# Second channel product of a ReLU-squared attention and MLP-mixer kernel: from one product per token tile to seven block products per two tiles (Strassen)

## The chip, the cores and the metric

The kernel runs on one core of one Trainium2 chip. The core has TensorE (PE, matrix products from on-chip memory SBUF into the accumulator PSUM, eight banks), VectorE (DVE), ScalarE (ACT), GpSimd (POOL, which here issues the loads) and SyncE (SP, which here issues stores and the DMA transposes), and 16 DMA engines. Each engine works through its own queue in order and waits on semaphores. The metric is the device time of the whole kernel in microseconds; lower is better.

## The reference

q, k and v are 8 batches x 12 heads x 448 tokens x 64. With them the reference computes

```python
scores = scale * np.matmul(q, k.transpose(0, 1, 3, 2))     # scale = 1/sqrt(64)
attn = np.maximum(scores, 0.0) ** 2 / S                     # S = 448
x = np.matmul(attn, v), heads side by side                  # 8 x 448 x 768
h = np.maximum(x.transpose(0, 2, 1) @ w_tok1, 0.0) @ w_tok2 # token mixing, 448 -> 256 -> 448
u = x + h.transpose(0, 2, 1)
h2 = np.maximum(u @ w_ch1, 0.0) @ w_ch2                     # channel mixing, 768 -> 1536 -> 768
out = u + h2                                                # float32
```

## The kernel before

The work goes in steps s = 0 to 23, one per batch b and group of four heads (three steps per batch). All 8 x 448 = 3584 tokens make 28 token tiles of 128, seven for every two batches (bb counts these pairs of batches). The products are in bf16 with float32 accumulation.

*Attention of a step.* GpSimd loads k, q and v (`ldk`, `ldq`, `ldv`, two DMAs each) into `raws`, four buffers of each. k and q are turned by TensorE up to step 9 (`T`), and from step 10 on by DMA: VectorE copies k or q into a buffer of `sides` (`ik`, `iq`; two buffers, so a copy waits for the transpose of two steps before), and SP issues a DMA transpose from there into `kqT` (`xk`, `xq`). For each of seven chunks c of 64 keys TensorE makes scores (`S`, two banks), ScalarE or VectorE takes the relu out of the banks into one of 13 buffers `sq` (`r`), VectorE squares it in place (`q`), and TensorE adds the value product (`V`, two banks held over all seven chunks). The result goes to `xT` (`xe`).

*Token mixing of a step.* From step 5 on SP turns `xT` into `x_sb` with a DMA transpose (`xd`); TensorE makes the first product (`t1`), ScalarE its relu (`rt`), TensorE the second (`t2`), and VectorE adds x to give u (`u`), which is kept channel-first in `uT_sb`, one buffer for two batches, two buffers in turn. SP turns u with DMA transposes into `u_sb`, token-first (`ub`), for use as the residual; `ub` is left out for batch 0, whose residual TensorE adds to the product with an identity matrix (`RESPE = {0}`, L572).

*Channel mixing.* The first product (`C1.b.e`, L517) is made for one batch and one of 12 blocks e of 128 hidden channels, six matmuls of 448 columns; ScalarE writes its relu to `r2_sb` (`c1e`), which holds two batches and exists twice. The second product (`C2.bb.t.i`, L568) takes one token tile t and a half i of the 768 output channels, 12 matmuls of 384 columns in one bank, one for each e; VectorE adds `u_sb` to it into one of three `out_sb` (`c2e`, L584), and SP stores the tile in two DMAs (`st`). The last tile goes in three parts.

*What sets the order.* `ORDER` is one long list of these names. The program emits them in that order, so every engine's queue holds its own operations in the list's order; a suffix `:A` or `:D` puts a step on ScalarE or VectorE, and digits name PSUM banks. The list had been worked out ahead of time. The first channel product of the later batches and most second products serve as TensorE's work beside the attention; about 80 us at the end consist of channel products alone.

Of the kernel before, what the change touches and what calls it, by code (L numbers as in the profile page):

```python
# [7 lines left out]
BF16 = mybir.dt.bfloat16  # L8
# [4 lines left out]
HOLD = 1  # L13
NSIDE = 2
FUSED = set()
RESPE = {0}
# [44 lines left out]
ldf.0 ident ldf.1 ldk0.1 ldk0.0 ldq1.1 ldk1.0 cast0.0:D cast0.1:A wt1.0 ldv1.0 ldq1.0 cast1.0:D cast1.1:A  # L61
ldk1.1 ldk2.1 fill:1*15 T0.0:0 ldv0.1 T0.1:1 cp0.0:A ldv0.0 cp0.1:D ldq2.1 fill:4*6 S0.4:23 S0.2:45 S0.5:67
ldv1.1 r0.4.0:A r0.4.1:D S0.1:01 r0.2.0:A r0.2.1:D ldk2.0 S0.0:23 r0.5.0:A r0.5.1:D ldq2.0 S0.3:45 r0.0.0:A
q0.2:D r0.0.1:A S0.6:67 ldk4.0 q0.4:D r0.1.0:A T1.0:23 ldq4.0 r0.1.1:A r0.3.0:D r0.3.1:A ldk4.1 q0.0:D cp1.0:A
cp1.1:D ldq4.1 r0.6.0:A q0.1:D S1.2:01 V0.0:45 ldk3.1 r0.6.1:A q0.3:D V0.1 r1.2.0:A V0.2 S1.1:32 q0.5:D wt1.1
S1.0:67 r1.2.1:A V0.3 q0.6:D V0.4 r1.0.0:A ldq3.1 V0.5 S1.5:01 q1.2:D r1.0.1:A V0.6 wt2 r1.1.0:A r1.1.1:D
S1.4:67 xe0.0:A xe0.1:D ldv2.1 r1.5.0:A q1.0:D r1.5.1:A ldv2.0 T2.0:32 q1.1:D r1.4.0:A V1.0:45 ldq3.0 r1.4.1:A
q1.5:D V1.1 S1.3:01 cp2.0:A cp2.1:D ldk3.0 X0.0:6 q1.4:D r1.3.0:A S1.6:72 wc1.0 X0.1:3 r1.3.1:A xc0.0:D
xc0.1:D r1.6.0:A S2.0:06 ldk5.1 q1.3:D S2.1:13 r1.6.1:A ldq5.0 r2.0.0:A r2.0.1:D S2.5:72 V1.2 r2.1.0:A q1.6:D
V1.3 S2.3:06 r2.1.1:A V1.4 r2.5.0:D V1.5 r2.5.1:A t1.0.0:1 q2.0:D r2.3.0:A V1.6 S2.4:37 q2.1:D r2.3.1:A  # L70
T4.0:20 ldv5.0 xe1.0:A xe1.1:D ldq5.1 rt0.0:A t1.0.1:6 q2.3:D r2.4.0:A ldv3.1 S2.2:45 r2.4.1:A cp4.0:D X1.1:1
ldk5.0 rt0.1:A cp4.1:D S2.6:37 r2.2.0:A V2.0:26 ldv3.0 V2.1 xc1.1:D r2.2.1:A T3.0:04 q2.4:D r2.6.0:A q2.2:D
r2.6.1:A X1.0:1 t1.1.1:5 cp3.0:A q2.5:D V2.2 S4.2:37 q2.6:D V2.3 xc1.0:A V2.4 V2.5 cp3.1:D V2.6 rt1.1:A
r4.2.0:A t1.1.0:0 r4.2.1:D xe2.0:A t2.0.1:1 xe2.1:D t2.1.1:5 rt1.0:A u0.1:D X2.0:4 S3.4:37 xc2.0:A u1.1:D
S3.3:26 wc1.1 t2.0.0:0 r3.4.0:A r3.4.1:D X2.1:1 t2.1.0:4 r3.3.0:A ldv4.0 u0.0:D t1.2.0:5 r3.3.1:A xc2.1:D
ldq7.0 S3.5:37 u1.0:D rt2.0:A S3.6:20 S3.0:61 r3.5.0:A ldq8.0 r3.5.1:D t2.2.0:5 r3.6.0:A S3.1:43 q3.3:D ldk7.0
r3.6.1:A t1.2.1:7 u2.0:D r3.0.0:A C1.0.2a:2 ldk6.0 rt2.1:A q3.4:D r3.0.1:A t2.2.1:0 ldv5.1 q3.5:D r3.1.0:A
C1.0.0a:6 r3.1.1:A u2.1:D ldv4.1 C1.0.1a:5 q3.0:D q3.1:D C1.0.2 q3.6:D S4.4:71 c1e0.2:A S4.3:43 q4.2:D
C1.0.4:0 r4.4.0:A r4.3.0:A r4.4.1:D r4.3.1:A C1.0.0 q4.4:D c1e0.4:A S3.2:27 q4.3:D T5.0:41 c1e0.0:A r3.2.0:A
r3.2.1:D S4.1:30 C1.0.1 cp5.0:A cp5.1:D C1.0.3:6 q3.2:D c1e0.1:A r4.1.0:A r4.1.1:D ldq7.1 V3.0:27 c1e0.3:A  # L80
S5.4:14 q4.1:D V3.1 ldq6.0 S4.5:53 S5.0:06 V3.2 r4.5.0:A r4.5.1:D V3.3 ldq6.1 V3.4 r5.0.0:A V3.5 r5.0.1:D
S5.2:53 V3.6 ldk6.1 r5.4.0:A r5.4.1:D C1.0.5:0 xe3.0:A xe3.1:D ldk7.1 r5.2.0:A q5.0:D r5.2.1:A C1.0.11:6 wc2.1
q4.5:D c1e0.5:A q5.2:D wc2.0 X3.0:1 c1e0.11:A q5.4:D S4.0:42 S5.1:75 wc2.2 xc3.0:D S4.6:30 r4.0.0:A C1.0.10:6
r4.0.1:A r5.1.0:D ldv6.1 r4.6.0:A r5.1.1:D ldv6.0 r4.6.1:A t1.3.0:1 q4.0:D c1e0.10:A ldv7.1 q5.1:D C1.0.6:4
# [573 lines left out]
```

## Time and profile before

| | before |
|---|---|
| three runs, median (lowest to highest) | 369.79 us (366.51 to 371.76) |
| span of the profiled execution | 368.3 us |
| mean granted TensorE clock | 0.989 |
| DMA traffic | 49.84 MB, mean 135 GB/s |
| squares, L422, VectorE | 168 x 618 ns, 97.1 us busy |
| relus of scores, ScalarE and VectorE | 227 and 109, 108.7 and 63.8 us busy |
| output adds, L584, VectorE | 51, 27.9 us busy |
| relus of the first channel product, ScalarE | 95 x 549 ns, 52.1 us busy |
| DMA transposes by SP: u, k and q, x | 42, 28, 19 |

A busy time is the union of an engine's instructions, so a group's mean is longer than the distance between two of its instructions that follow each other at once; the distance is read from the starts in a timeline. A busy share is an average over stages with different limits, so stages are read apart.

### The profile page before, as it was taken

The numbers are of one execution on the slowest core, as the hardware profiler recorded it, in microseconds if no ns is written. First come the engines' busy times: TensorE is split into PE (matmuls) and PEld (weight loads), VectorE is DVE, ScalarE is ACT, GpSimd is POOL, SyncE is SP. The second block draws the span as 40 slices with busy tenths as digits, with TensorE's granted clock in tenths as the row PEclk, the third lists the DMA queues.
The fourth block names the chain that finished last, engine by engine and source line by source line (L and its number), as shares of the span: only waits on it lengthen the run. The fifth ranks groups of instructions, "written<-read, shape, count | busy, mean of one in ns | idle before, by whom it ended". The sixth has DMA issues, their size and how long they took to land.

```text
span 368.3 us, 8763 instructions
## 1 busy us (share of the span) xinstructions
PE 355.3 (96%) x3564; PEld 198.8 (54%) x3564; DVE 245.8 (67%) x458; ACT 189.9 (52%) x388; POOL 91.3 (25%) x156
## 2 busy tenths in 40 slices
PE   7789999999999799999999999999999999999995
PEld 4455455565655355555555555555545565555564
DVE  3996999979389575989477997988588213201222
ACT  4996888548374356746164765566366122122200
POOL 9865532415154032133033033301000000000000
PEclk9998999999999989999999999999999999999999
DMA  8999999949999979999999599999141511511435
GB/s 152 175 184 190 189 182 179 143 100 136 154 181 147 190 126 154 170 134 182 225 116 197 105 145 157 189 165 190 32 89 26 118 44 25 134 43 25 104 85 130
DMA packets 96073, 49.84 MB, mean 135 GB/s; under 512 B 69984, under 2 KB 92576, under 8 KB 96032
## 3 DMA queue, kind: packets, MB, share of 16 engines
q1 hardware_dynamic: 71440, 27.61, 42.8%
q0 software_dynamic: 24352, 21.47, 42.7%
q8 instruction: 28, 0.46, 0.5%
q10 hardware_dynamic: 240, 0.20, 0.2%
q14 instruction: 13, 0.11, 0.1%
HBM read 43.38 MB, written 11.01 MB: 148 GB/s over the span
## 4 chain that ended last, share of the span: by engine, by line
PE 90%; DMA 4%; DVE 3%; issue 1%; ACT 1%; POOL 0%; POOLq 0%; ACTq 0%
PE m_ps L517 30%; PE m_ps L568 29%; PE sc_ps L412 9%; PE acc_ps L439 9%; PE t_ps L483 6%; PE h_ps L492 5%; DMA x_sb<-xT 3%; DVE sq L422 2%; PE kqT_ps L371 1%; DMA k_raw<-in_k_dram 1%; DVE sq L251 1%; PE x_ps L474 1%; DVE kqT L257 0%; ACT sq L249 0%; PE m_ps L572 0%
## 5 line engine op out<-in xcount | busy, mean ns | idle before, releaser
L249 ACT ACTIVATE sq<-sc_ps 128x448 bf16<-128x448 f32 x227 | 108.7, 570 | 30.4 <-PE sc_ps L412 27.9
L517 PE MATMUL m_ps<-uT_sb,wc 128*128 128x448 bf16 x576 | 119.0, 353 | 0.0
L568 PE MATMUL m_ps<-wc,r_sb 128*128 128x384 bf16 (+2 forms) x684 | 117.2, 323 | 0.0
L249 ACT ACTIVATE r_sb<-m_ps 128x448 bf16<-128x448 f32 x95 | 52.1, 549 | 102.1 <-PE m_ps L517 101.9
L422 DVE TENSOR_TENSOR sq<-sq 128x896 bf16<-128x896 bf16 x168 | 97.1, 618 | 0.9 <-ACT sq L249 0.2
L568 PEld LDWEIGHTS <-r_sb 128*128 128x128 bf16 x684 | 65.6, 98 | 45.3 <-issue 2.9
L517 PEld LDWEIGHTS <-wc 128*128 128x128 bf16 x576 | 54.6, 98 | 53.2 <-issue 6.8
L584 DVE TENSOR_TENSOR out_sb<-m_ps,u_sb 128x384 f32<-128x384 f32 (+2 forms) x51 | 27.9, 548 | 72.5 <-PE m_ps L568 61.5
L251 DVE TENSOR_SCALAR sq<-sc_ps 128x448 bf16<-128x448 f32 x109 | 63.8, 618 | 16.5 <-PE sc_ps L412 8.9
L271 POOL DMA_DIRECT2D v_raw<-in_v_dram x48 | 29.2, 616 | 121.7 <-PE sc_ps L412 64.7
L412 PE MATMUL sc_ps<-kqT 64*64 64x448 bf16 x672 | 55.9, 360 | 1.9 <-ACT kqT L255 1.7
L439 PE MATMUL acc_ps<-sq,v_raw 64*64 64x448 bf16 x672 | 49.0, 362 | 1.0 <-ACT sq L249 0.4
L271 POOL DMA_DIRECT2D q_raw<-in_q_dram x46 | 28.5, 632 | 28.8 <-PE kqT_ps L371 19.9
L496 DVE TENSOR_TENSOR uT_sb<-h_ps,xT 128x448 bf16<-128x448 f32 x48 | 29.0, 618 | 8.1 <-PE h_ps L492 7.8
L412 PEld LDWEIGHTS <-kqT 64*64 64x64 bf16 x672 | 20.8, 106 | 23.0 <-issue 13.4
L271 POOL DMA_DIRECT2D k_raw<-in_k_dram x48 | 29.6, 631 | 3.0 <-DMA wc<-in_moe_w_ch_dram 1.1
L439 PEld LDWEIGHTS <-v_raw 64*64 64x64 bf16 x672 | 21.2, 109 | 14.4 <-issue 6.1
L483 PE MATMUL t_ps<-x_sb,wt 128*128 128x256 bf16 (+1 forms) x216 | 26.6, 269 | 2.4 <-DMA x_sb<-xT 2.4
L483 PEld LDWEIGHTS <-wt 128*128 128x128 bf16 x216 | 19.5, 101 | 10.1 <-DMA x_sb<-xT 2.8
L492 PE MATMUL h_ps<-wt,r_sb 128*128 128x448 bf16 x96 | 24.6, 354 | 0.0
L249 ACT ACTIVATE r_sb<-t_ps 128x512 bf16<-128x512 f32 (+1 forms) x27 | 15.5, 575 | 14.4 <-PE t_ps L483 14.3
L451 DVE TENSOR_SCALAR xT<-acc_ps 128x448 bf16<-128x448 f32 x24 | 14.8, 619 | 1.6 <-PE acc_ps L439 1.6
(39 smaller groups left out, 109.4 us busy)
## 6 DMA issues: line engine op xcount, KB each, us to landing
out_dram<-out_sb SPq DMA_DIRECT2D x54, 192.0 KB, 3.1
k_raw<-in_k_dram POOLq DMA_DIRECT2D x48, 112.0 KB, 6.2
v_raw<-in_v_dram POOLq DMA_DIRECT2D x48, 112.0 KB, 5.4
q_raw<-in_q_dram POOLq DMA_DIRECT2D x46, 112.0 KB, 6.4
wc<-in_moe_w_ch_dram POOLq DMA_DIRECT2D x2, 1152.0 KB, 10.7
wc<-in_moe_w_ch_dram POOLq DMA_DIRECT2D x3, 768.0 KB, 12.9
u_sb<-uT_sb SPq DMA_TRANSPOSE x42, 4.0
side<-in_q_dram SPq DMA_DIRECT2D x2, 224.0 KB, 3.4
```

The lines of the kernel that those rows point to most:

```text
L249: nc.scalar.activation(out, ps, AF.Relu)
L251: nc.vector.tensor_scalar(out=out, in0=ps, scalar1=0.0, scalar2=None, op0=ALU.max)
L271: nc.gpsimd.dma_start(out=raws[t][s % NR][64 * half:64 * (half + 1)], in_=src[b, h0:h0 + 2].rearrange('e (p c) d -> p e (c d)', c=KC))
L412: nc.tensor.matmul(o.ps[e][64 * half:64 * (half + 1), :S], lhsT=lhsT, rhs=rhs, start=True, stop=True, skip_group_check=True)
L422: sq_ops[s, c] = [add(Op(f'q{s}.{c}', 'DVE', lambda o: nc.vector.tensor_tensor(out=buf, in0=buf, in1=buf, op=ALU.mult), ev))]
L439: nc.tensor.matmul(o.ps[half][64 * e:64 * (e + 1), :S], lhsT=r[rows, e, c * D:(c + 1) * D], rhs=sq[rows, e, :], start=c == 0, stop=c == KC ...
L483: nc.tensor.matmul(o.ps[:, j, :], lhsT=wt1[:, c, j * 128:(j + 1) * 128], rhs=x_sb[:, p0:p1, c, :], start=c == 0, stop=c == 3)
L492: nc.tensor.matmul(o.ps[:, :S], lhsT=r1[:, j, a * 128:(a + 1) * 128], rhs=wt2[:, j, :], start=j == 0, stop=j == JC - 1)
L496: nc.vector.tensor_tensor(out=uTs[bb % 2][:, 2 * i + a, off:off + S].rearrange('n (c p) -> n c p', c=KC), in0=t2.ps[:, :S].rearrange('n (p ...
L517: nc.tensor.matmul(ps[:, :S], lhsT=wc1[:, g, e * 128:(e + 1) * 128], rhs=uT[:, g, off:off + S], start=g == 0, stop=g == CC - 1)
L568: nc.tensor.matmul(o.ps[:, :size], lhsT=r2[:, e, t * 128:(t + 1) * 128], rhs=wc2[:, e, cols], start=e == 0, stop=e == EC - 1)
L584: nc.vector.tensor_tensor(out=out_sb[:, cols].rearrange('n (g d) -> n g d', d=128), in0=u.ps[:, :size].rearrange('n (g d) -> n g d', d=128 ...
```

## The change

The second channel product takes two token tiles at a time (14 pairs p). Let A be the pair's rows of `r2`, as blocks A11, A12 (first tile; first and second half of the 1536 hidden channels), A21 and A22 (second tile), and B11 to B22 the four blocks of w_ch2, 768 x 384 each. Strassen's scheme in Winograd's form makes the four output blocks from seven products of a block by a block (`P1` to `P7`), six matmuls of 384 columns each. It needs

- four sums of blocks of A for each pair, on VectorE in bf16, 128 x 768 elements each: S1 = A21 + A22, S2 = S1 - A11, S4 = A12 - S2 in the buffers `sums`, and S3 = A11 - A21 written over A21;
- four sums of blocks of B, once, on VectorE in eight pieces (`ws`);
- seven adds into `out_sb` for each pair (`a`, `b`, `c`, `f21`, `f11`, `f22`, `f12`) where there were four. P1, P6, P7 and P4 accumulate in one bank, which VectorE reads after each of them; `a`, `b`, `c` and `f21` add u from `u_sb`, the other three add P2, P5 and P5 + P3 to what is in `out_sb`.

`r2` and `u_sb`, which were two buffers of seven tiles each, become rings of eleven tiles (`RING`). A batch whose tokens run over the ring's end is evicted in two pieces (`c1e` of batches 3 and 6), and its `ub` transposes are issued in two pieces too. The residual of batch 0 now comes through `ub` as well. To make room, `sides` goes from two to one (`NSIDE`; a copy now waits for the transpose of the step before), `sq` from 13 to 10 (`NSQ`), v's buffers from four to three; `out_sb` goes from three to four; the warm-up operand lies in an `out_sb`, and B12 in `sums`. w_ch2 is loaded in four blocks rather than three parts. `ORDER` is worked out anew, so every operation may stand at another place, and some evictions move between ScalarE and VectorE. There are 28 start-up filler matmuls where there were 21.

```diff
-HOLD = 1
-NSIDE = 2
-FUSED = set()
-RESPE = {0}
+HOLD = 3
+NSIDE = 1
+RING = 11
+NSUM = 6
...
-    NR, NQ, NSQ, NX, NO = (4, 3, 13, 3, 3)
+    EH = EC // 2
+    RT = RING * 128
+    NQ, NSQ, NX, NO = (3, 10, 3, 4)
+    NR = {'k': 4, 'q': 4, 'v': 3}
...
-    wc2 = sbuf.tile([128, EC, DM], BF16, name='wc2')
+    wc2 = {w: sbuf.tile([128, EH, HN], BF16, name=f'wc2_{w}') for w in ('11', '21', '22', 't1', 't2', 't3', 't4')}
+    sums = sbuf.tile([128, NSUM, EH, 128], BF16, name='sums')
+    wc2['12'] = sums[:, 0:3].rearrange('p a e n -> p (a e n)').rearrange('p (e n) -> p e n', e=EH)
...
-    u_sbs = [sbuf.tile([128, CC, NT, 128], BF16, name=f'u_sb{i}') for i in range(2)]
-    r2s = [sbuf.tile([128, EC, 2 * S], BF16, name=f'r2_sb{i}') for i in range(2)]
+    u_sb = sbuf.tile([128, CC, RING, 128], BF16, name='u_sb')
+    r2 = sbuf.tile([128, EC, RT], BF16, name='r2_sb')
...
+    def weight_sums():
+        for h in range(2):
+            e = slice(h * EH // 2, (h + 1) * EH // 2)
+            for w, x, y in (('t1', '12', '11'), ('t3', '22', '12'), ('t2', '22', 't1'), ('t4', '21', 't2')):
+                deps = [wc2_ops[z] if z in wc2_ops else wsum[z, h] for z in (x, y)]
+                wsum[w, h] = add(Op(f'ws{w[1]}.{h}', 'DVE', lambda o, w=w, x=x, y=y, e=e: nc.vector.tensor_tensor(out=wc2[w][:, e], in0=wc2[x][:, e], in1=wc2[y][:, e], op=ALU.subtract), deps))
...
+                for t0, t1, slot in ((lo, cut, first), (cut, hi, 0)):
+                    if t0 < t1:
+                        x = nc.sync.dma_start_transpose(out=u_sb[:, g, slot:slot + t1 - t0, :], in_=uTs[bb % 2][:, g, t0 * 128:t1 * 128])
...
+        def evict(o):
+            for x, y, z in ((0, cut, at), (cut, S, 0)):
+                if x < y:
+                    relu(o, r2[:, e, z:z + y - x], u.ps[:, x:y])
...
+        sum1 = summed('s1', s1, block(1, 0), block(1, 1), ALU.add, ready(1, 0) + ready(1, 1) + old)
+        sum3 = summed('s3', block(1, 0), block(0, 0), block(1, 0), ALU.subtract, ready(0, 0) + [sum1])
+        sum2 = summed('s2', s2, s1, block(0, 0), ALU.subtract, [sum1] + ready(0, 0) + old)
+        sum4 = summed('s4', s4, block(0, 1), s2, ALU.subtract, [sum2] + ready(0, 1) + old)
...
+                for e in range(EH):
+                    nc.tensor.matmul(banks[into][:, :HN], lhsT=lhs[:, e], rhs=wc2[w][:, e], start=after is None and e == 0, stop=e == EH - 1, skip_group_check=True)
...
+        p1 = product(1, block(0, 0), '11', ready(0, 0), 'x')
+        a = added('a', 0, 0, 'x', [p1], True)
+        p6 = product(6, s2, 't2', [sum2], 'x', a)
+        b = added('b', 0, 1, 'x', [p6], True)
+        p7 = product(7, block(1, 0), 't3', [sum3], 'x', b)
+        c = added('c', 1, 1, 'x', [p7], True)
+        p4 = product(4, block(1, 1), 't4', ready(1, 1), 'x', c)
+        f21 = added('f21', 1, 0, 'x', [p4], True)
+        p2 = product(2, block(0, 1), '21', ready(0, 1), 'y')
+        f11 = added('f11', 0, 0, 'y', [p2, a], False)
+        p5 = product(5, s1, 't1', [sum1], 'z')
+        f22 = added('f22', 1, 1, 'z', [p5, c], False)
+        p3 = product(3, s4, '22', [sum4], 'z', f22)
+        f12 = added('f12', 0, 1, 'z', [p3, b], False)
```

More of the change, by code (lines that the diff above doesn't have):

```diff
@@ L417, in score @@
         old = vals[divmod(n - NSQ, KC)] if n >= NSQ else None
-        if (s, c) in FUSED:
-            sq_ops[s, c] = [add(Op(f'z{s}.{c}.{e}', 'DVE', lambda o, e=e: nc.vector.scalar_tensor_tensor(out=buf[:, e], in0=u.ps[e][:, :S], scalar=0.0, in1=u.ps[e][:, :S], op0=ALU.max, op1=ALU.mult), [u, old])) for e in range(2)]
-            return u
         ev = [add(Op(f'r{s}.{c}.{e}', 'ACT', lambda o, e=e: relu(o, buf[:, e], u.ps[e][:, :S]), [u, old])) for e in range(2)]
```

437 lines of the change are left out of this document (223 added, 214 removed).

## Prediction

> **What bounds the kernel now.** I read the head of the page, then the chain of waits, then the busy time by stage, since the shares of the whole span average over an attention part and a tail that have different limits.
>
> ```profile
> span 368.3 us, 8763 instructions
> ...
> PE 355.3 (96%) x3564; PEld 198.8 (54%) x3564; DVE 245.8 (67%) x458; ACT 189.9 (52%) x388; POOL 91.3 (25%) x156
> ...
> PE 90%; DMA 4%; DVE 3%; issue 1%; ACT 1%; POOL 0%; POOLq 0%; ACTq 0%
> PE m_ps L517 30%; PE m_ps L568 29%; PE sc_ps L412 9%; PE acc_ps L439 9%; PE t_ps L483 6%; PE h_ps L492 5%; DMA x_sb<-xT 3%; DVE sq L422 2%; PE kqT_ps L371 1%; DMA k_raw<-in_k_dram 1%; DVE sq L251 1%; PE x_ps L474 1%; DVE kqT L257 0%; ACT sq L249 0%; PE m_ps L572 0%
> ```
>
> TensorE (PE) carries 90% of the chain, and the second channel product (L568) alone 29%: the stage that the change shortens is on the path. By stage (columns: busy time of PE, its weight loads, VectorE, ScalarE, GpSimd; granted clock; DMA share):
>
> ```profile
> 0.00:30.00 30.00, 23.54 (x502) 14.13 (x506) 22.20 (x46) 23.12 (x47) 22.18 (x41) 0.98 1.08 172
> 30.00:285.50 255.50, 252.71 (x2589) 138.56 (x2590) 206.17 (x380) 152.64 (x316) 69.13 (x115) 0.99 1.01 149
> 285.50:364.40 78.90, 78.90 (x479) 46.15 (x477) 17.06 (x31) 14.15 (x26) 0.00 (x0) 1.00 0.33 78
> ```
>
> The cut at 285.5 us is where the last x transposes (xd22, xd23) are issued. After it PE is full and VectorE has 17.06 of 78.90; before it PE is full too, but VectorE is already at 206.17 of 255.50 (81%), and the DMA engines at 1.01. So the tail has room for VectorE work, the attention part little.
>
> **The change part by part.** Rates first, from starts in PE's timeline, since a group's own duration overlaps its successor:
>
> ```profile
> 282.35 2.06 PE L439 MATMUL acc_ps<-sq,v_raw 64*64 64x448 bf16 x40
> 284.34 1.31 PE L517 MATMUL m_ps<-uT_sb,wc 128*128 128x448 bf16 x6
> ...
> 287.44 2.43 PE L517 MATMUL m_ps<-uT_sb,wc 128*128 128x448 bf16 x12
> 289.70 0.54 PE L492 MATMUL h_ps<-wt,r_sb 128*128 128x448 bf16 x2
> 290.08 7.96 PE L568 MATMUL m_ps<-wc,r_sb 128*128 128x384 bf16 x48
> 297.88 1.04 PE L483 MATMUL t_ps<-x_sb,wt 128*128 128x256 bf16 x8
> 298.76 2.43 PE L517 MATMUL m_ps<-uT_sb,wc 128*128 128x448 bf16 x12
> ```
>
> A 384-column matmul takes (297.88 - 290.08)/48 = 0.1625 us, a 448-column one (289.70 - 287.44)/12 = 0.188, a t1 group 0.88, a t2 group 0.38, and four quadrant matmuls of a V step (284.34 - 282.35)/10 = 0.20.
>
> *TensorE.* Before: 28 token tiles x 2 halves x 12 = 672 matmuls. After: 14 pairs x 7 products x 6 = 588. That is 84 x 0.1625 = 13.65 us less. The residual by identity goes, and seven start-up fills come:
>
> ```profile
> L572 PE MATMUL m_ps<-ident,uT_sb 128*128 128x128 bf16 x18 | 2.0, 219 | 0.0
> L627 PE MATMUL fill_ps<-warm 128*128 128x128 bf16 x21 | 1.5, 220 | 0.0
> ```
>
> At a third of 0.1625 a 128-column matmul is 0.054, so the 18 give 1.0 (at most the 2.0 of the row) and the fills take 0.4, in a stretch where PE waits anyway. TensorE's sum: -14.3. The order moves first channel groups too: with 20 after xd23 where there were 23 (3 x 6 x 0.188 = 3.4 us), and 42 products (42 x 6 x 0.1625 = 41.0) for 25 groups of the old form (25 x 12 x 0.1625 = 48.8), the tail is 78.9 - 11.2 = 67.7 us long. So most of the gain lies in the tail, and before xd23 PE has only 3 us less.
>
> *VectorE.* Its back-to-back rate:
>
> ```profile
> 278.36 0.55 DVE L584 TENSOR_TENSOR out_sb<-m_ps,u_sb 128x384 f32<-128x384 f32 x1
> 278.84 0.62 DVE L251 TENSOR_SCALAR sq<-sc_ps 128x448 bf16<-128x448 f32 x1
> 279.38 1.69 DVE L422 TENSOR_TENSOR sq<-sq 128x896 bf16<-128x896 bf16 x3
> ```
>
> An output add of 384 takes 0.48, a relu of 448 from PSUM 0.54, and so does a square ((1.69 - 0.62)/2). Adds go from 56 to 98: +42 x 0.48 = 20.2. The sums of r2 blocks (bf16, SBUF, 768 elements) stand in no row; the nearest is the square of 896: between 0.46 (by proportion) and 0.54, and I take 0.48: 56 x 0.48 = 26.9. Eight weight sums of 1152 elements: 0.54 x 1152/896 = 0.69 each, 5.5. Moves between VectorE and ScalarE come to -3.8. Together +48.8, of which 29.5 before xd23: (206.17 + 29.5)/255.5 = 92%, beside a PE at 98%. After it VectorE has some 35 of 67.7 us and is covered.
>
> What 92% costs two in-order engines I bound by pieces. I cut each order list into ten equal parts, count both engines' work by the rates above, and sum the larger. Before it is 342.2 (PE's own sum 334.2); after it is 335.3 (PE 319.9). In the new parts one to six VectorE leads or ties: 22.5, 27.0, 25.9, 30.8, 30.7, 30.0 against 13.5, 23.4, 24.6, 29.7, 30.7, 29.5. So of 14.3 only 342.2 - 335.3 = 6.9 is left: VectorE gives back 7.4. Bounds: 0 (it hides behind the waits that the 368.3 - 342.2 us between sum and span hold) and 14.3 (all).
>
> *The x transposes.* xd copies xT into x_sb through SP's queue, t1 on PE waits for it, and everything on PE queues behind t1.
>
> ```profile
> L462 SPq DMA_TRANSPOSE x_sb<-xT x19: 1231/1303/3438, 63.0 to 286.8; - x19
> DMA to landing us min/median/max: 3.1/6.8/13.2
> ...
> DMA to landing us min/median/max: 3.1/3.2/3.3
> ```
>
> (The last row is for 260 to 290 us, when no loads run.) In the old order the work between xd and t1, the larger of PE and VectorE, is 8.0 us at least; in the new one it is 5.9, 5.5, 5.9, 6.2, 5.4 and 5.4 for steps 5, 10, 12, 13, 17, 20. At a landing of 6.8 the shortfalls sum to 6.5; at 3.2 to nothing. The k and q loads go out earlier (from step 10 on 13 us of work or more before use, where 6.6 was the least), which thins the DMA queue at those places, but the v loads still start beside xd. I take 3, bounds 0 and 6.5 here. One such wait is in the trace:
>
> ```profile
> 116.79 10.64 DMA x_sb<-xT
> ...
> 122.64 2.43 PE L517 MATMUL m_ps<-uT_sb,wc 128*128 128x448 bf16 x12
> 127.47 1.68 PE L483 MATMUL t_ps<-x_sb,wt 128*128 128x256 bf16 x8 [2.40 <-DMA x_sb<-xT]
> ...
> 126.00:128.00 2.00, 0.53 (x4) 0.45 (x5) 0.00 (x0) 0.00 (x0) 0.00 (x0) 0.93 1.16 296
> 128.00:130.00 2.00, 2.00 (x18) 1.02 (x20) 0.00 (x0) 0.60 (x1) 0.00 (x0) 0.50 1.17 253
> ```
>
> After 2.40 us of waiting the granted clock (the column before the DMA share) was 0.50 for 2 us, so a wait of that length costs 1 us or more beyond itself. The Trainium skill (TensorE: Matmul & The Clock Gate, What's actually happening) puts the drop to half only after an idle window of about 3.4 us; by that none of these short waits would cost extra, which the row contradicts.
>
> *The rest*, each at nothing. Wrapped evictions of batches 3 and 6 add 24 ScalarE instructions of at most 0.55 (the row's mean), 13 us beside an idle ScalarE (some 100 us in the middle stage); were it not idle, the block sums would start late by as much. SP gets 18 more u transposes, 1.2 us of issue each, spread out; the six new ones of batch 0, held for a piece of wc2, could delay an xd queued behind them. Squares in a ring of ten and v in one of three make relus and v loads wait for value steps that lie three, or one head group, nearer; PE is ahead of both. A bank's chain of four products and three adds has another group between its links. The store rings (four tiles) leave 3.2 us at the tightest, just over the median landing; the tail's idle VectorE covers it.
>
> ```profile
> L249 ACT ACTIVATE r_sb<-m_ps 128x448 bf16<-128x448 f32 x95 | 52.1, 549 | 102.1 <-PE m_ps L517 101.9
> L504 SPq DMA_TRANSPOSE u_sb<-uT_sb x42: 1177/1218/2444, 64.7 to 318.7; - x42
> ...
> DMA to landing us min/median/max: 1.9/2.9/6.4
> ```
>
> Sum: 368.3 - 14.3 + 7.4 + 3 = 364.4, say **364 us**. The profiled span lies inside the three runs (366.51 to 371.76), 1.5 under their median of 369.79; I set no offset on top. Two per cent of that median, about what a measurement of this kernel can tell from no change, is 362.4 to 377.2: the forecast is 1.6% below, within it.
>
> **The rivals.**
>
> *VectorE hides.* Returned 0 to 3 and no wait for x: 354 to 357, say 355. For it: the tail's 11.2 us cannot be lost, and the old span holds 26 us of slack over its own sum. Against: the five parts in which VectorE's work exceeds PE's.
>
> *Slower: x_sb lands late.* In the case above (step 8) the transpose took 10.64 us, the counted work beside it was 10.1, and yet PE waited 2.40 and not 0.5: what counts may be landing plus 2, or 8.8. Then the shortfalls of steps 5 to 20 sum to 23.8 in place of 3: 364.4 + 20.8 = 385. From 8.0 on (sum 16) it passes 377. For it: landings to 13.2. Against: one such wait in the old run, and thinner loads.
>
> *The single side buffer.* Crossing copies now wait for the transpose just before, not the one before that, and VectorE's relus, squares and adds queue behind them.
>
> ```profile
> DMA to landing us min/median/max: 3.0/4.9/11.6
> DVE side L390 <- DMA kqT<-side: 5.7, 1, 5.7
> ```
>
> The order leaves 5.2 us or more: nothing lost at 4.9. At half as long again, 7.3, the shortfalls of twelve copies sum to 17; half of that on the path makes 372.
>
> *It does not do what it says:* the strided r2 blocks, summed at one element a cycle. By the relu's and the add's rows 64 elements cost 0.06, so 768 cost 0.84, not 0.48: 34 x 0.36 = 12 us more before xd23, 376.
>
> **How the numbers follow.** Forecast (360 to 369) 0.42; VectorE hides 0.26; side buffer 0.13; late x_sb 0.14; slow sums 0.05. Faster by over 2%: 0.26 and a good quarter of the forecast's own range, 0.38. Slower: most of late x_sb and some of the slow sums, 0.12. Within: 0.50. The range of eight in ten reaches from 354 to 376: below lies little of the second case, above the late x_sb.
>
> **What would show it.** Right: some 84 fewer matmuls in the second product's group at an unchanged 0.16 us; a tail of about 68 us; VectorE at nine tenths from 40 to 250 us, with short PE waits on VectorE and x_sb. Wrong: PE waits on x_sb above 10 us in total; VectorE waiting for kqT; sums with a mean far over 0.56; or an attention part that ends well before 285 us, in which case VectorE hid.

## The result and the profile after

The changed kernel takes 388.58 us in the median of five runs (384.86 to 393.18); the kernel before, run beside it, took 371.76 us (366.51 to 372.54). The ratio is 1.044, with a 95% interval of 1.033 to 1.054: slower by 4%, where 1.6% faster was forecast, and above the forecast's range of 354 to 376. Every ratio here leaves out the runs that lie more than 1.5% above the fastest of their kernel (two of these five), so it is not the quotient of the medians. The profiled execution of the changed kernel has a span of 386.8 us (before 368.3) and a mean granted clock of 0.966 (before 0.989).

The page's head after the change, with PE's busy tenths, the granted clock and the DMA share in 40 slices of 9.7 us, and the chain of waits by engine and by line:

```profile
span 386.8 us, 8706 instructions
...
PE 350.7 (91%) x3457; PEld 192.0 (50%) x3457; DVE 292.5 (76%) x557; ACT 195.6 (51%) x418; POOL 92.4 (24%) x157
...
PE   7786999967919997998999999999999999999994
...
PEclk9998799996978998999999999999999999999998
DMA  8999983999999899999899996799153372521335
...
PE 65%; DMA 19%; DVE 6%; ACT 5%; issue 3%; POOL 0%; DVEq 0%; ACTq 0%; POOLq 0%
PE m_ps L584 22%; PE m_ps L533 21%; DMA kqT<-side 10%; DMA x_sb<-xT 7%; PE sc_ps L420 6%; PE acc_ps L444 6%; PE t_ps L488 5%; PE h_ps L497 4%; DVE sq L427 3%; ACT sq L252 3%; DVE sq L254 1%; DMA k_raw<-in_k_dram 1%; ACT kqT L258 1%; PE kqT_ps L379 0%; ACT xT L454 0%
```

PE is busy for 4.6 us less than before, but its idle time went from 368.3 - 355.3 = 13.0 us to 386.8 - 350.7 = 36.1. PE's row shows where: the digits fall in slices 9, 10, 12 and 16 (77 to 97, 106 to 116 and 145 to 155 us). DMA carries 19% of the chain where it carried 4%, 17 of it in two kinds of DMA transposes, those of k and q and those of x. The lower clock adds, by estimate, 0.034 x 386.8 - 0.011 x 368.3 = 9 us. So the forecast's 14.3 us less work, 23.1 us more idle time and 9 us of clock give 17.8; the spans differ by 18.5.

Stages, cut as the prediction cut them (the last x transposes are now issued at 313.9 us):

```profile
0.00:30.00 30.00, 24.06 (x451) 12.04 (x452) 22.62 (x47) 23.61 (x48) 25.11 (x46) 1.00 1.07 160
30.00:313.90 283.90, 258.83 (x2609) 140.97 (x2610) 232.84 (x440) 158.77 (x339) 67.25 (x111) 0.96 0.96 137
313.90:381.80 67.90, 67.81 (x401) 39.03 (x399) 36.57 (x72) 13.17 (x32) 0.00 (x0) 1.00 0.36 87
```

The tail is 67.9 us long, as forecast (67.7). The whole loss, and more, is in the middle: 283.9 us where the old order took 255.5. Inside it one stretch stands out. The same 60 us, first of the kernel before, then of the changed one (PE, its weight loads, VectorE, ScalarE, GpSimd; clock, DMA share, GB/s):

```profile
60.00:120.00 60.00, 59.61 (x656) 33.69 (x656) 48.96 (x90) 35.01 (x71) 21.38 (x36) 1.00 1.16 144
```

```profile
60.00:120.00 60.00, 45.22 (x494) 23.77 (x493) 42.52 (x79) 31.34 (x64) 21.68 (x35) 0.89 1.19 146
```

PE loses 14.4 us there and a tenth of its clock, at the same DMA traffic. The chain of waits of the changed kernel in this stretch names the cause of most of it:

```profile
75.34 14.24 DMA x_sb<-xT
89.59 0.05 issue
89.63 1.89 PE t_ps L488 x8
...
100.52 14.32 DMA x_sb<-xT
114.84 0.05 issue
114.88 1.89 PE t_ps L488 x8
```

Twice (steps 6 and 8) an x transpose lands 14.3 us after its issue; PE runs out of other work and stands still for 5.98 and 8.71 us, and the t1 group after it takes 1.89 us instead of 0.88, which is half clock. The waits of the whole run (us in total, times, longest):

```profile
DVE side L398 <- DMA kqT<-side: 17.9, 7, 9.1
...
PE t_ps L488 <- DMA x_sb<-xT: 14.7, 2, 8.7
DVE sq L254 <- PE sc_ps L420: 14.1, 6, 8.1
```

And the x transposes on SP's queue, with their landing:

```profile
L467 SPq DMA_TRANSPOSE x_sb<-xT x19: 1232/1300/4279, 65.2 to 313.9; - x19
...
DMA to landing us min/median/max: 3.2/4.4/14.4
```

The median landing has fallen, from 6.8 to 4.4, and the worst has risen from 13.2 to 14.4: not all transposes are slower, a few are, and they now stand where PE has nothing else.

A landing is counted from the issue, and the issue itself came late. SP works through its queue in order, and from 72 to 115 us that queue is nearly always busy (its lines stand in the last section). The x of step 7 was ready at 84.98 us, when the second of its evictions ended, and its transpose was issued at 92.18, behind five u transposes. The x of step 8 was ready at 97.09 and was issued at 100.52, behind two u transposes.

### The profile page after: what moved, and what is told of

Its sections match the earlier page's. It is cut to its first block, busy times and chain, and to the rows that moved or that the text cites. A ratio compares the mean times of both kernels' runs of the same rounds, so it can differ in the third digit from the quotient of the medians.

```text
span 386.8 us, 8706 instructions
## 1 busy us (share of the span) xinstructions
PE 350.7 (91%) x3457; PEld 192.0 (50%) x3457; DVE 292.5 (76%) x557; ACT 195.6 (51%) x418; POOL 92.4 (24%) x157
## 4 chain that ended last, share of the span: by engine, by line
PE 65%; DMA 19%; DVE 6%; ACT 5%; issue 3%; POOL 0%; DVEq 0%; ACTq 0%; POOLq 0%
PE m_ps L584 22%; PE m_ps L533 21%; DMA kqT<-side 10%; DMA x_sb<-xT 7%; PE sc_ps L420 6%; PE acc_ps L444 6%; PE t_ps L488 5%; PE h_ps L497 4%; DVE sq L427 3%; ACT sq L252 3%; DVE sq L254 1%; DMA k_raw<-in_k_dram 1%; ACT kqT L258 1%; PE kqT_ps L379 0%; ACT xT L454 0%
## 5 line engine op out<-in xcount | busy, mean ns | idle before, releaser
L252 ACT ACTIVATE r_sb<-m_ps 128x448 bf16<-128x448 f32 (+2 forms) x116 | 51.7, 474 | 106.5 <-PE m_ps L533 105.7
L254 DVE TENSOR_SCALAR sq<-sc_ps 128x448 bf16<-128x448 f32 x109 | 63.7, 617 | 14.7 <-PE sc_ps L420 14.1
L444 PE MATMUL acc_ps<-sq,v_raw 64*64 64x448 bf16 x672 | 59.9, 360 | 1.9 <-DVE sq L427 1.4
L599 DVE TENSOR_TENSOR out_sb<-m_ps,u_sb 128x384 f32<-128x384 f32 x56 | 30.9, 553 | 25.0 <-PE m_ps L584 23.0
L488 PE MATMUL t_ps<-x_sb,wt 128*128 128x256 bf16 (+1 forms) x216 | 27.6, 275 | 18.9 <-DMA x_sb<-xT 14.7
L584 PEld LDWEIGHTS <-r_sb 128*128 128x128 bf16 x336 | 32.6, 98 | 23.6 <-issue 1.4
L420 PEld LDWEIGHTS <-kqT 64*64 64x64 bf16 x672 | 25.9, 106 | 28.4 <-issue 18.4
L584 PEld LDWEIGHTS <-sums 128*128 128x128 bf16 x252 | 24.9, 100 | 19.6 <-issue 3.3
L601 DVE TENSOR_TENSOR out_sb<-m_ps,out_sb 128x384 f32<-128x384 f32 x42 | 23.1, 553 | 14.9 <-PE m_ps L584 14.7
L584 PE MATMUL m_ps<-wc_t,sums 128*128 128x384 bf16 x168 | 32.8, 339 | 0.0
L274 POOL DMA_DIRECT2D q_raw<-in_q_dram x46 | 28.0, 624 | 18.1 <-DVE side L398 11.8
L584 PE MATMUL m_ps<-wc,r_sb 128*128 128x384 bf16 x168 | 31.2, 326 | 0.0
L584 PE MATMUL m_ps<-wc_t,r_sb 128*128 128x384 bf16 x168 | 30.6, 326 | 0.0
```

Source lines behind the costliest of these rows:

```text
L252: nc.scalar.activation(out, ps, AF.Relu)
L254: nc.vector.tensor_scalar(out=out, in0=ps, scalar1=0.0, scalar2=None, op0=ALU.max)
L274: nc.gpsimd.dma_start(out=raws[t][s % NR[t]][64 * half:64 * (half + 1)], in_=src[b, h0:h0 + 2].rearrange('e (p c) d -> p e (c d)', c=KC))
L420: nc.tensor.matmul(o.ps[e][64 * half:64 * (half + 1), :S], lhsT=lhsT, rhs=rhs, start=True, stop=True, skip_group_check=True)
L444: nc.tensor.matmul(o.ps[half][64 * e:64 * (e + 1), :S], lhsT=r[rows, e, c * D:(c + 1) * D], rhs=sq[rows, e, :], start=c == 0, stop=c == KC ...
L488: nc.tensor.matmul(o.ps[:, j, :], lhsT=wt1[:, c, j * 128:(j + 1) * 128], rhs=x_sb[:, p0:p1, c, :], start=c == 0, stop=c == 3)
```

## The experiments

Seventeen kernels were run, each against the kernel before on the same chip. Where nothing else is said, the edit is of the changed kernel. Its own span is 386.8 us. A span is that of one execution, and those of the changed kernel went from 383.1 to 391.4 us, so a gain of 3 or 4 us against it is not told from scatter. The first question was whether late transposes or VectorE's new sums are to blame (theories A and B), the second what makes the transposes late.

| kernel | median us | ratio to before (95%) | span us |
|---|---|---|---|
| changed kernel | 388.58 | 1.044 (1.033 to 1.054) | 386.8 |
| nosums | 388.68 | 1.052 (1.044 to 1.060) | 384.9 |
| light_before | 365.66 | 0.989 (0.985 to 0.994) | 363.9 |
| light_after | 361.90 | 0.983 (0.977 to 0.989) | 358.2 |
| light_nosums | 364.11 | 0.987 (0.980 to 0.993) | 362.2 |
| x_free | 378.34 | 1.033 (1.020 to 1.046) | 375.0 |
| side_free | 401.85 | 1.091 (1.080 to 1.102) | 397.8 |
| both_free | 397.58 | 1.080 (1.070 to 1.091) | 395.4 |
| wc2_early | 385.21 | 1.043 (1.030 to 1.057) | 383.7 |
| t1_late | 390.91 | 1.059 (1.048 to 1.070) | 388.1 |
| both_late | 394.56 | 1.066 (1.052 to 1.080) | 394.6 |
| loads_late | 394.25 | no interval | none used |
| light_early | 367.76 | 0.994 (0.988 to 1.000) | none used |
| u01_free | 374.93 | 1.017 (1.007 to 1.027) | 375.0 |
| x_on_pe | 379.24 | 1.029 (1.018 to 1.040) | 377.1 |
| xkq_on_pe | 374.81 | 1.017 (1.007 to 1.027) | 373.2 |
| xkq_wc2 | 372.81 | 1.010 (1.002 to 1.018) | 374.3 |
| xkq_wc2_spread | 376.01 | 1.016 (1.007 to 1.025) | 374.0 |

### VectorE's sums: nosums, light_nosums

```diff
-            return add(Op(f'{name}.{p}', 'DVE', lambda o: nc.vector.tensor_tensor(out=out, in0=x, in1=y, op=op), deps))
+            return None
...
-        p6 = product(6, s2, 't2', [sum2], 'x', a)
+        p6 = product(6, block(0, 0), 't2', ready(1, 0) + ready(1, 1) + ready(0, 0), 'x', a)
```

(P7, P5 and P3 likewise; light_nosums has the edit of light_after besides.)

> The changed kernel with all loads but without the four block sums of each pair (second channel product not the reference's). Theory A: the x and kqT waits stay, a few us gained, 380 to 386. Theory B: 27 us of VectorE work less, of which 16 lie before the tail: 370 or less.

> The changed kernel without those loads and without the four block sums of each pair (56 VectorE instructions of some 0.48 us; the products read blocks of r2 in their place, so the second channel product is not the reference's). If VectorE's share gives back 7 us, as forecast, this is 7 us below the run without loads alone; if VectorE hides, the same as that; if VectorE is the real limit, 20 us below it.

Without the 56 block sums the span is 384.9 for 386.8 us, and with the loads of the later steps left out as well it is 362.2 for 358.2. So the sums cost nothing that can be measured, with or without loads. They are as short as forecast: of 128 x 768 elements each (minimum, median and maximum in ns),

```profile
L571 DVE TENSOR_TENSOR sums<-r_sb x14: 547/548/559, 104.6 to 367.7; 128x768 bf16<-128x768 bf16 x14
```

and two that follow each other start 0.47 us apart. Theory B falls.

### Without the loads of the later steps: light_after, light_before

```diff
-            load(s, t)
+            load(s, t) if s < 6 else loads.setdefault((s, t), [])
```

> The changed kernel without the loads of k, q and v from step 6 on (the buffers keep what steps 2 to 5 left, so those steps are computed from older heads): the DMA transposes, SP's queue, the order and all work of the engines stay, two thirds of the loaded bytes go. Theory A (transposes that land late beside loads make the loss): about 362, the forecast without its 3 us for x. Theory B (VectorE's work and in-order queues make it): 378 or more. A jam of SP's own transposes, whatever is loaded: x still lands after 10 us and more, above 380.

> The kernel before without the loads of k, q and v from step 6 on, as a control. Its trace has one wait for x of 2.4 us with 1.7 us of half clock behind it, so by theory A it gains about 4 us (368.3 to 364), and the changed kernel without loads would come out 2 to 4 us below it; by theory B it gains the same 4 us and stays well below the changed one.

The changed kernel gains 28.6 us of span, the kernel before 4.4. With these loads gone the change is faster, as was forecast of its arithmetic: 358.2 against 363.9 us of span, a gain of 5.7. By the medians of the two it is 3.8 us, since the profiled execution of light_after was the fastest of its four. In light_after the x transposes land like this:

```profile
L467 SPq DMA_TRANSPOSE x_sb<-xT x19: 1231/1233/1317, 61.7 to 284.9; - x19
...
DMA to landing us min/median/max: 3.0/3.2/5.1
```

All issues take some 1.2 us of SP, the landings lie between 3.0 and 5.1, and the last x transposes are issued at 284.9 us (313.9 with all loads). PE itself waits for loads for only 1.0 us in the changed kernel, so the loss is transposes that are late beside loads. Open was what makes them cost more in the new order than in the old.

### Taking one wait away: x_free, side_free, both_free, wc2_early

```diff
-        x_sb = x_sbs[s % 2]
+        x_sb = x_sbs[s % 2 if s < XDMA else 0]
...
-            ready = add(Op(f'xd{s}', 'SP', lambda o: nc.sync.dma_start_transpose(out=x_sb.rearrange('p a c d -> p (a c) d'), in_=xTs[s % NX].rearrange('p a n -> p (a n)')), xe[s] + old))
+            ready = add(Op(f'xd{s}', 'SP', lambda o: nc.sync.dma_start_transpose(out=x_sbs[1].rearrange('p a c d -> p (a c) d'), in_=xTs[s % NX].rearrange('p a n -> p (a n)')), xe[s] + old))
```

> The changed kernel, but from step 5 on t1 reads a fixed x_sb (the one that step 4 left) while the xd transposes go on as before into the other x_sb: the DMA traffic and SP's queue stay, only PE's wait for x goes, and token mixing of steps 5 to 23 is computed from step 4's x. Theory A (late DMA transposes, with the half clock after each long wait, make the 20 us over the forecast): the two waits of 6.0 and 8.7 us and the clock dips behind them go, 386.8 - 14.7 - 4 = about 368 us. Theory B (VectorE is the limit, and the x waits only cover its backlog): less than 5 us gained, 383 us or more.

The span falls by 11.8 us, between the two theories and less than the waits and the half clock behind them, since PE now stands still at the other kinds of transposes: once for kqT, and for 4.5 us behind output adds, of which one waited 6.0 us for a u transpose. A wait of x_free:

```profile
PE sc_ps L420 <- DMA kqT<-side: 6.9, 1, 6.9
```

In side_free the k and q transposes read the raw buffers, to take VectorE's wait away:

```diff
-                nc.sync.dma_start_transpose(out=kqTs[s % NQ][:, j].rearrange('p (c n) -> p c n', c=KC), in_=side[:, j].rearrange('p c n -> p (c n)'))
+                nc.sync.dma_start_transpose(out=kqTs[s % NQ][:, j].rearrange('p (c n) -> p c n', c=KC), in_=raws[t][s % NR[t]].rearrange('p e n -> p (e n)'))
```

> The changed kernel, but the xk and xq transposes read the raw k and q buffers in place of the side buffer (the copies into it are still made, nobody reads them), so VectorE's copies never wait for a transpose; scores of steps 10 to 23 are computed from k and q in another layout. Theory A: VectorE's 17.9 us of waits for kqT go, but 9.1 of them lie under the 8.7 us x wait, so 4 to 8 us are gained, about 381. Theory B: VectorE's own time being the limit, all 17.9 us come back, about 370. If the single side buffer costs nothing on the path: 387.

> The edits of the two runs before together (token mixing from a fixed x_sb, scores from the raw buffers). Theory A: the forecast without its 3 us for x, 361, give or take 4. Theory B: VectorE's 92% still stops PE in turn, 375 or more.

Both became slower, by 11 and 8.6 us of span, and tell nothing of the side buffer: the raw buffers are now held until the transposes land, so loads wait for transposes. A line of side_free:

```profile
POOL q_raw L274 <- DMA kqT<-q_raw: 41.7, 5, 17.2
```

In wc2_early the four words `wc2.*` of ORDER stand ahead of `ldv7.0`.

> The changed kernel with one change of order: the four loads of w_ch2 stand ahead of the v loads of step 7 in GpSimd's queue, some 10 us earlier, where the DMA engines move 80 to 110 GB/s. If these 2.3 MB are what makes the x transpose of step 6 land after 14.2 us, its wait of 6.0 us, the half clock behind it and VectorE's idle 8.1 us go, and the second wait (step 8) stays: 8 us less, 379. If the jam is in SP's own queue of u transposes: no change, 387.

Its span is 3.1 us shorter, which is within the scatter; the x waits still come to 11 us, now in part for step 5. The place of the w_ch2 loads alone is not the cause.

### More work between a transpose and its reader: t1_late, loads_late, both_late

Only ORDER is edited, so there is no short diff: in t1_late the words `t1`, `rt`, `t2`, `u` of eleven steps stand later; in loads_late the words `ldk` and `ldq` of steps 10 and on; in both_late both, and `ik`, `iq` too.

> Changed kernel, only the order edited: the t1 groups of steps 5, 6, 8, 10 to 15, 17 and 20 (and the r, t2, u work behind them) stand later, so that at least 7 to 10 us of other TensorE work lie between the issue of an x transpose (xd) and the t1 that reads it. Nothing is left out. Theory A1 (the new order leaves the transposes too little work to hide behind; the landings are what they are): the x waits (14.7 us in the changed kernel) fall to about 6 or less, as the landings of 14.3 us still exceed 10 by 4 twice; span 370 to 378. Theory A2 (the loads and transposes as a whole take the queues, so that a wait taken away comes back at the next transpose): the x waits fall but waits behind kqT (17.9 us on VectorE, 14.1 on sq) grow; span 380 to 387.

> Changed kernel, only the order edited: the k and q loads of steps 10 and later are issued about 12 us of TensorE work ahead of the copy that reads them, in place of the bursts in which the new order issues them. The t1 groups stand where they stood. Nothing is left out. Theory A2b (bursts of loads are what makes single transposes land at 14 us): the largest x landing falls from 14.4 to about 9, the x waits from 14.7 to under 7; span 372 to 380, that is 7 to 15 below the changed kernel. Theory A1 (margins): the span stays at 384 to 390, or rises where a load now lands late (POOL's k_raw and q_raw and VectorE's side copies would then wait for loads).

> Changed kernel, only the order edited: t1 later as in t1_late, the side copies (iq, ik) of steps 10 and later at least about 8 us after the transposes of the step before, and the k and q loads about 14 us of work ahead of the copies. Nothing is left out. Theory A (transposes that land late are the whole of the loss; light_after gives 358 as the floor without the loads): span 362 to 372, ratio 0.97 to 1.01 to the kernel before. If the lateness only moves: VectorE's sums, which the order puts after the moved work, come late and the tail grows; span 378 to 388.

None is faster: spans of 388.1 (t1_late) and 394.6 us (both_late), and a median of 394.25 for loads_late. In t1_late the x waits hardly fall (12.7 us for 14.7) and VectorE's waits for kqT stay (18.6): PE waits just as long, 9.87 us at 114 us of the run:

```profile
113.93 1.89 PE L488 MATMUL t_ps<-x_sb,wt 128*128 128x256 bf16 x8 [9.87 <-DMA x_sb<-xT]
```

and in the 60 us from 60 on it gets through 46.25 us where the changed kernel had 45.22:

```profile
60.00:120.00 60.00, 46.25 (x511) 23.68 (x510) 43.06 (x80) 31.59 (x64) 22.41 (x36) 0.91 1.21 147
```

SP's queue shows why the added distance did not help at this wait:

```profile
91.54 3.91 SPq L467 DMA_TRANSPOSE x_sb<-xT  x1
95.49 6.01 SPq L513 DMA_TRANSPOSE u_sb<-uT_sb  x2
101.61 3.82 SPq L467 DMA_TRANSPOSE x_sb<-xT  x1
```

The x of step 8 was ready at 93.35 us, and its transpose (the last line) was issued at 101.61, behind the transpose of step 7 and two u transposes. PE was done with the work in between at 104.05. So most of the distance that the order put in was used up before the issue, and the run does not test what a distance from the issue would do. t1_late lies above the range of A1 (margins) and three of the four runs of loads_late above that of A2b (bursts of loads); A2, that the queues as a whole are taken, comes nearest; whether the queue of SP or the rate of the DMA engines is the limit is not shown by them. (Three runs of loads_late took 394.19 to 395.78 us and one 380.3, so no ratio is given.)

### The rate: what the DMA engines have to do from 60 to 132 us

What the new order asks of the DMA engines, first the kernel before, then the changed one, each from 60 to 120 us (queue: packets, MB, share; then issues with median landing):

```profile
q0 software_dynamic: 5270, 4.22, 59.8%
q1 hardware_dynamic: 13230, 4.31, 56.0%
...
u_sb<-uT_sb SPq DMA_TRANSPOSE x9, 7.3
x_sb<-xT SPq DMA_TRANSPOSE x5, 9.0
kqT<-side SPq DMA_TRANSPOSE x5, 9.1
```

```profile
q0 software_dynamic: 7168, 5.57, 68.5%
q1 hardware_dynamic: 12643, 3.08, 50.0%
...
wc<-in_moe_w_ch_dram POOLq DMA_DIRECT2D x3, 576.0 KB, 10.4
...
sums<-in_moe_w_ch_dram POOLq DMA_DIRECT2D x1, 576.0 KB, 18.3
u_sb<-uT_sb SPq DMA_TRANSPOSE x13, 11.4
x_sb<-xT SPq DMA_TRANSPOSE x4, 14.3
kqT<-side SPq DMA_TRANSPOSE x4, 6.8
```

The new order puts 1.35 MB more loads here (the w_ch2 blocks among them, which the old order loaded from 44 us on) and four more u transposes, though PE gets less far. Two rates make an estimate of it. In the first 30 us the loads run at 160 GB/s with all engines busy (the first row of the stages above). A transpose alone takes at most 1.06 us of all 16 engines: in light_after, from 76 to 122 us, q1 was busy for 53.1% of 46 us with 23 transposes and four stores:

```profile
q1 hardware_dynamic: 15952, 4.59, 53.1%
...
u_sb<-uT_sb SPq DMA_TRANSPOSE x12, 2.6
kqT<-side SPq DMA_TRANSPOSE x8, 3.0
x_sb<-xT SPq DMA_TRANSPOSE x3, 3.2
```

The work that the changed kernel does from 60 to 132 us (by the u adds of VectorE, the same ones) light_after does in 52 us, from 57 to 109. In those 72 us the changed kernel moved

```profile
q0 software_dynamic: 8032, 6.26, 65.2%
...
u_sb<-uT_sb SPq DMA_TRANSPOSE x16, 10.3
kqT<-side SPq DMA_TRANSPOSE x6, 6.8
x_sb<-xT SPq DMA_TRANSPOSE x4, 14.3
```

that is 6.26 / 0.16 = 39 us of loads and 26 x 1.06 = 28 us of transposes, 67 us of all engines for 52 us of other work. By the same rates the kernel before needs 26 + 20 us, and 7 for its six stores, for 60 us of work: it just fits. This is theory C, that the DMA engines' own time is the limit.

The sum is rough. While the transpose of step 6 was under way (75.34 to 89.58 us) the engines moved 178 GB/s, so 160 is no ceiling; while that of step 8 was (100.52 to 114.84) they moved 130, with as long a landing. For the second wait the bytes alone do not account.

### Theory C tested: light_early, u01_free

```diff
-            load(s, t)
+            loads.setdefault((s, t), []) if 6 <= s < 12 else load(s, t)
```

> Changed kernel without the loads of k, q and v of steps 6 to 11 (36 of 142; those of later steps stay), so those steps compute on old data; issued from about 30 to 110 us. Theory C (the DMA engines are full in one stretch: between 76 and 122 us the changed kernel moves 4.2 MB of loads, at the 0.16 MB a us of the first 20 us some 26 us of all engines, and 17 transposes of about 1.1 us, together some 44 of 46 us, and transposes can only land late): the two x waits (14.7 us) and the half clock behind them vanish, and most of the 28.6 us with them; span 362 to 370. Theory A1 (too little work between a transpose and its reader everywhere): only the share of the early steps goes; span 374 to 382.

The profiled execution of this kernel ran for 1210 us, far from its nine others (363.67 to 370.31), so only those are used. Their spans are 361.8 to 368.4 us, where theory C had 362 to 370: a third of the loads that light_after leaves out brings about 20 of its 28.6 us. The early loads are the ones that hurt.

```diff
-                    if t0 < t1:
+                    if t0 < t1 and b > 1:
```

> Changed kernel without the 12 u transposes of batches 0 and 1 (the residual of these two batches is a block of zeros; the sums and all else stay). Theory C: some 13 us of all DMA engines' time leave the stretch from 60 to 115 us and SP's queue is shorter by 12 issues of 1.3 to 4 us ahead of the x transposes of steps 6 to 8; these land under 10 us, the x waits fall from 14.7 to under 4; span 366 to 376. If the loads alone make the transposes late: x waits stay above 10, span 380 to 388.

Twelve u transposes less, with all loads in place, give 375.0 us of span, 11.8 less, and in the stretch

```profile
60.00:120.00 60.00, 53.68 (x575) 28.78 (x578) 50.17 (x93) 34.40 (x69) 24.12 (x39) 0.94 1.18 144
```

PE has 53.7 us for 45.2. By the estimate above 12 x 1.06 = 12.7 us of engine time is gone. The waits on x fall from 14.7 to 6.6, not under 4 as expected: in sum right, in the one wait too low. The twelve are those of batches 0 and 1; only batch 0's six are new with the change, since the old order has batch 1's as well. And they are twelve issues less in SP's queue too, so this run does not tell the engines' time from that queue. x_free, which took only the wait for x away and left every transfer, came to the same 375.0 us of span, with a median 3.4 us higher.

### A version that needs fewer DMAs there: x_on_pe, xkq_on_pe, xkq_wc2, xkq_wc2_spread

The program already turns x on TensorE up to step 4 and k and q up to step 9. Two numbers move these borders, and ORDER gets `X`, `xc` and `T`, `cp` in place of `xd` and `ik`, `iq`, `xk`, `xq`:

```diff
-XDMA, QDMA = (5, 10)
+XDMA, QDMA = (10, 13)
```

(x_on_pe has 10, 10.)

> Changed kernel with x of steps 5 to 9 transposed on TensorE as steps 0 to 4 have it (eight short matmuls of about 0.45 us together and a ScalarE copy of 0.6 us each) in place of the DMA transposes. Nothing is left out. Theory C and A: the waits on x of steps 6 and 8 go, 5 transposes leave the full stretch; cost 2.3 us of TensorE; as x_free, where only the wait went, gained 11.8 us of span, this gains 10 to 16; span 371 to 377, and part of the wait shows again at kqT of steps 10 to 12.

> As x_on_pe, and k and q of steps 10 to 12 too are transposed on TensorE as steps 0 to 9 have it (0.5 us a step, copies on ScalarE and VectorE) in place of VectorE's side copies and DMA transposes. Nothing is left out. Theory C: the full stretch loses 11 transposes and its waits on kqT (6.9 us in x_free) go; cost 4 us of TensorE; span 362 to 370, ratio 0.97 to 1.00 to the kernel before. If the wait only moves on to the transposes of steps 13 and later: span 371 to 377, no better than x_on_pe.

x_on_pe comes to 377.1 us of span, just above its range, and PE waits 5.1 us for kqT. xkq_on_pe comes to 373.2, 3 us above theory C's range and inside the one for a wait that moves on; VectorE indeed still waits 9.4 us for kqT, now of steps 13 and later. PE in the stretch of xkq_on_pe:

```profile
60.00:120.00 60.00, 57.25 (x791) 32.35 (x793) 51.76 (x94) 42.44 (x80) 24.21 (x40) 1.00 1.10 133
```

57.25 us busy at full clock (45.22 at 0.89 in the changed kernel), and in the whole run one wait of PE itself on a DMA transpose is left, of 0.7 us.

> As xkq_on_pe, and the four w_ch2 loads issued ahead of the loads of v of step 7, as in wc2_early, so that they fall into the stretch from 58 to 68 us, in which xkq_on_pe moves 0.35 MB where it moves 1.0 to 1.8 MB in the four slices of 10 us behind it. Nothing is left out. Theory C: 2.4 MB, some 15 us of loads, leave the full stretch; the 7 us that steps 8 and 9 still lose against light_after go in good part; span 366 to 371, level with the kernel before. If only the number of transposes mattered: span 371 to 375.

> As xkq_wc2, and the k and q loads of steps 13 to 17, which the new order issues up to 43 us of TensorE work ahead of their use, at most about 22 us ahead. Nothing is left out. Theory C: up to ten more loads (0.7 us of all engines each) leave the stretch from 100 to 112 us; span 362 to 369, ratio 0.97 to 1.00. If the early loads did no harm or the later ones now wait for VectorE's or POOL's queue: 370 to 378.

With the w_ch2 loads early as well the median is 372.8 us against 372.7 for the kernel before in the same call (ratio 1.010, 1.002 to 1.018): level within 2%, not better. The profiled execution (374.3 us of span) was the slowest of its six; the others have spans of 369.9 to 371.3, inside theory C's range, where xkq_on_pe has 372.3 to 373.8. That would be a gain of some 2 us, but the two were run on different chips and the intervals of their ratios overlap, so it is not shown. xkq_wc2_spread, with a median of 376.0 us and spans of 371.6 to 377.0, misses theory C's range. No version that does the whole work beats the kernel before.

## Why the prediction was wrong

- **TensorE's -14.3: nearly right.** L584 has 3 x 168 + 84 = 588 matmuls, 84 fewer, with a mean of 326 ns as in the old form (339 in one of the four rows, 326 there too in light_after). Without the later loads PE is busy for 353.0 us before and 340.8 after, 12.2 less.

- **The tail, 67.7 us: right** (67.9), with VectorE at 36.6 us in it and no wait on PE's path that matters.

- **VectorE gives back 7.4: not shown.** Without the sums nothing is gained (nosums, light_nosums). In the light pair the change wins 5.7 us of span (3.8 by the medians), against the 6.9 of the sum without x waits, and PE's idle time there grows by 17.4 - 10.9 = 6.5 us. That is near the size of the term, but of it 2.8 us are an x wait, and light_nosums shows that VectorE's sums are not the cause; the added output adds, the other part of VectorE's new work, were taken out in no run, and where the rest lies stays open.

- **The x transposes, 3 us, bounds 0 and 6.5: this step failed.** It took the landings of the old run (median 6.8) as a property of the transpose and asked only how much work the new order leaves beside each. The landings depend on what the same order puts on the queues, and the margin counts from an issue that SP's queue can hold back. With the loads in, the term is 14.7 us of wait, with half clock behind each, and what is not waited for at x is in part waited for at kqT. With the later loads out one wait of 2.8 us is left (light_after), and that it comes near the 3 is luck: by the prediction's margins a landing of 3.2 costs nothing. That transpose landed in 3.25 us, but its x was ready at 150.69 us and its issue came at 156.39, when the four u transposes ahead of it in SP's queue were out; PE had by then done nearly all of the work that was to lie beside it.

- **"SP gets 18 more u transposes ... at nothing": this step failed with it.** The step counted SP's issue time at 1.2 us each and named the six of batch 0 as a possible delay, but put that at nothing. In the full stretch an issue takes up to 4.3 us, and the transposes of x stood up to 7.2 us ready behind u transposes. Neither what these take of the DMA engines nor that the w_ch2 blocks come later into the same stretch was counted. u01_free puts twelve u transposes at 11.8 us, six of them new; no run takes out the new ones alone.

- **"The k and q loads go out earlier, which thins the DMA queue": not borne out.** It held for the median landing, not in the full stretch; but moving these loads later did not help either (loads_late, xkq_wc2_spread).

- **The rival "x_sb lands late" (385 us, chance 0.14) came out** in its place, its sign and nearly its time, but not by its rule of landing plus 2 at six steps: two landings of 14.3 us at steps 6 and 8 did most of it, and neither step is among the six that the prediction lists. The prediction's own signs of being wrong both appeared: x waits above 10 us (14.7) and VectorE waiting for kqT (17.9 us where it was 5.7).

- **The side buffer** could not be tested by itself; side_free changed who holds the raw buffers. That VectorE waits for it in the changed kernel is seen; what it costs is open.

- **The clock row held in part.** After waits of 5.98 and 8.71 us the t1 group ran at half speed (1.89 us for 0.88), as it did, in 1.68 us, after 2.40 us in the old run. But after 2.77 us in light_after and 2.80 us in t1_late it took 1.03 and 1.05 us, at a granted clock of 1.00, so a wait of that length does not always cost more than itself. The waits of 5.98 and 8.71 us also agree with the window of about 3.4 us of the Trainium skill (TensorE: Matmul & The Clock Gate, What's actually happening), so they do not decide between the two; the 2.77 and 2.80 us agree with it as well, and the 2.40 us of the old run still stands against it.

What stays open is why these transposes are late. That the loads beside them are needed for it is shown by light_after and light_early. That the DMA engines' own time is the limit rests on the rough sum of 67 us for 52 and on the edits that take loads or transposes out of the stretch and gain (light_early, u01_free, x_on_pe, xkq_on_pe). Against it, x_free left all transfers in and gained nearly as much as u01_free, moving the loads alone (wc2_early, loads_late) gained nothing that stands out of the scatter, and the second wait fell in a stretch of 130 GB/s. SP's in-order queue is the rival that no run tests by itself: the runs with fewer transposes shorten it too. And light_after with the added TensorE work (5 x 0.45 + 3 x 0.5 = 3.8 us) would give 362 us of span, where xkq_wc2 has 369.9 to 374.3: 8 to 12 us have no named cause (light_after's own spans go from 358.2 to 361.3).

## What to carry to other kernels

A new issue order moves the DMAs too: before trusting landings from the old trace, compare what each stretch of the new order asks of the DMA engines, and of the queue that issues the transfers, with the compute in that stretch. When a transpose is late, look first at when its source was ready and when it was issued: a longer distance in the order is no help if the transpose stands behind others in its queue meanwhile. A transpose that an idle share of TensorE and ScalarE can do is worth taking off the queues where they are full, even when TensorE is the bound elsewhere.

## What the runs showed of the hardware

- A DMA transpose of x landed 3.2 us after its issue in the median of light_after, without the later loads, and up to 14.4 us after it beside loads in the changed kernel. Its issue on SP stretched with it, from 1.23 us to 4.28, which held up whatever SP had to issue next. SP's queue in the changed kernel:

```profile
79.38 12.69 SPq L513 DMA_TRANSPOSE u_sb<-uT_sb  x5
92.18 3.90 SPq L467 DMA_TRANSPOSE x_sb<-xT  x1
96.12 4.29 SPq L513 DMA_TRANSPOSE u_sb<-uT_sb  x2
100.52 4.28 SPq L467 DMA_TRANSPOSE x_sb<-xT  x1
```

- The mean granted clock falls with PE's waits: 0.966 in the changed kernel, 0.989 in xkq_on_pe, the same matmuls but for 3.8 us, and 0.997 in light_after (0.986 to 0.990 in its other runs). With 23 us more idle time than before, the lower clock cost by estimate another 9.
- Waits of nearly the same length were followed by half clock or not: after 2.40 us a t1 group took 1.68 us (the kernel before), after 2.77 and 2.80 us it took 1.03 and 1.05 (light_after, t1_late).
